# Attention and a PReLU layer on one core: alpha's load moved ahead of the second key load, one more tile stored token by token

## The chip, the core and the metric

The kernel runs on one core of a Trainium2 chip. A core has TensorE (PE: matrix multiplies and weight loads), VectorE (DVE), ScalarE (ACT), GpSimd (POOL) and SyncE (SP). Each engine works through its own list of instructions in order; between engines semaphores say when a result is there. SP and ACT also issue DMAs, the transfers between the chip's memory (HBM) and the core's memory (SBUF). PE writes its results to PSUM, eight banks of 128 x 512 float32, from which DVE and ACT fetch them.

The metric is the time of one execution in microseconds (us), measured on the device. Names with a number after a point, such as h9.10, are the kernel's own names for its steps and are explained below.

## What is computed

First comes attention with polynomial features: per row x, `phi(x)` is the outer product of two 8-vectors, S1 x and S2 x, 64 numbers. Its result, turned into 4352 tokens of 128 numbers, goes through two matrices with a PReLU between them.

```python
def phi(x):                                   # q, k, v: (4, 4, 1088, 32)
    a = np.einsum('rd,bhsd->bhsr', S1, x)     # S1, S2: (8, 32)
    b = np.einsum('rd,bhsd->bhsr', S2, x)
    return np.einsum('bhsi,bhsj->bhsij', a, b).reshape(*x.shape[:-1], r * r)
q_p, k_p = (phi(q), phi(k))
kv = np.einsum('bhsf,bhsd->bhfd', k_p, v)
z = np.sum(k_p, axis=2)
num = np.einsum('bhsf,bhfd->bhsd', q_p, kv)
den = np.einsum('bhsf,bhf->bhs', q_p, z)[..., None] + 1e-06
attn = num / den
x = attn.transpose(0, 2, 1, 3).reshape(4352, 128)
h = x @ w_in                                  # w_in: (128, 2048), alpha: (2048,)
g = np.maximum(h, 0.0) + alpha * np.minimum(h, 0.0)
out = g @ w_out                               # w_out: (2048, 128)
```

## The kernel before

**Stages.** Each of the four batches has a keys part and a queries part. Keys of batch 0: the key rows come in two loads (k0.0 of 18 rows per partition, k0.1 of 16), DVE transposes them (k0T0, k0T1, line 439), PE multiplies them by the features (k0f0, k0f1, line 473) with a weight tile `Wk` that DVE makes from S1 and S2, DVE turns the result back (k0fT1, k0fT0, line 477), POOL and DVE form the products (k0p0 to k0p4), and PE sums them: over the rows alone (zs00, zs01, line 504) and against v (kv00 to kv04, line 513). The sum zs goes through ACT (z10) and a small matmul (zS0, line 413) with the weight tile `S2q`, which itself is S2m on PE (line 329) and four ACT instructions (line 335); DVE then writes C0 into the weights of the queries. The queries of batch 0 are three pieces, qa0, qa1 (rows 0 to 15) and qb (the rest).

**The start.** Both S1 and S2 (1 KB each, into the tile `rows`) are needed before anything but transposes can run: rowsT (line 316) turns them on PE, DVE makes `Wk` and k0f0 follows. alpha (8 KB, tile `al`) is turned on PE by alT (line 340), much later.

**The second half.** x is cut into tiles: 0 and 1 of 256 tokens, 2 to 8 of 512, and tile 9 of 256 with the left-over tokens of all batches. For each tile g and each of 16 chunks c: h{g}.{c} is a matmul with a piece of `w_in` into a PSUM bank (line 628), r{g}.{c} is the relu from PSUM into a bfloat16 tile `rh`, on ACT (line 634) or DVE (line 636), and o{g}.{c} multiplies it by a piece of `w_out` scaled by 1 - alpha and sums over c in one bank. W{g} adds the linear part, x times w_in alpha w_out. A plain tile does o as one matmul of 512 columns with `w_a_bf` as weights (line 621); its result lies features by tokens, DVE transposes it in blocks of 32 (oT, line 654), and four stores st{g}.0 to .3 write 128-byte rows (line 664). Tile 8 is token-major: `rh` is the weight, four matmuls of 128 columns do the work (line 619), two copies of 256 columns (oT8.0, oT8.1) fetch it from PSUM, and four stores write 512-byte rows. Tile 9 does the same in two halves (line 616), with its own stores st9.0 to st9.2 from the tiles `of`.

**What sets the order.** Nothing is scheduled when the kernel is built: the table ORDER lists each step by name with its engine (p, a, d, g, s) and the PSUM banks or buffers it takes. A number behind p is a count of units of dummy work ahead of the step: `dummy` (line 294) issues matmuls of ones into bank 7, up to four units of 128 columns each, for no result. They fill PE while it waits.

**Waits of DMAs.** The DMAs of SP and ACT take eight completion semaphores, DMAHW0 to DMAHW7, in turn, in one order for both engines. A DMA that takes a semaphore first waits until the DMA that held it last, eight DMAs back, has landed. A DMA that waits holds up the queue of its engine.

```python
n = len(loads.setdefault(name, []))
o = op({e: 440 for e in eng}, emit, deps, name=f"ld_{name}" + (f"_{n}" if n else ""), nbytes=nbytes, rate=rate)
```

So `ld_rows` is S1, `ld_rows_1` is S2, and the four loads of v0 are ld_v0, ld_v0_1 to ld_v0_3, of which ld_v0_1 is issued last. SP's first DMAs are S2, S1, qb, w_in2, qa1, v0_3, v0, qa0, v0_2, v0_1.

Of the kernel before, what the change touches and what calls it, by code (L numbers as in the profile page):

```python
# [21 lines left out]


ORDER = """
ld_rows_1:s ld_rows:s ld_k0.0:a ld_k0.1:a ld_qb:s ld_alpha:a zero:d table:a ident:g identb:d selP:g ld_w_in2:s wz:g rowsT:p26:0 pads:g M2:d k0T0:d:0
Wk:d k0f0:p8:1 k0T1:d pads9:g Mh:d win2:a ld_qa1:s qbT:d ld_v0_3:s ld_v0:s M4:d k0f1:p1 k0fT1:d:0 k0fT0:d k0p0:g:0 zs00:p15:1 zs01:p ld_qa0:s ld_v0_2:s
z10:a:0 k0F1:d:2 k0p4:d S2m:p:3 S2q:a zS0:p15 qaT1:d qaT0:d ld_v0_1:s Wq:d k0p1:g ld_k2:s k0p2:d ld_w_out2:s C0:d alT:p:3 oma:d kv00:p1:4 alTc:a Wf:a
qcf:p:1 w_b2:g kv01:p kv02:p k0p3:d qcfc:a:0 qct:d:0 kv03:p kv04:p ld_w_in1:s qcrc:d:0 qcb:d qcp0:d:0 ld_w_in0:s ld_w_in3:s kvc0:a:0 qcPT0:d:0 qbf:p:2
qdf:p:0 qdfc:a:1 fin0:p kvR0:a ld_w_out1:s ld_k1:s qbfc:a:0 ld_k1_1:s w_a2:g ld_w_out0:s qdt:d:0 ld_k2_1:s win1:a win0:a ld_w_out3:s ld_q1_1:s ld_q1:s
# [33 lines left out]
r7.1:a:2 o8.11:p h7.12:p:2 st0.2:s o8.7:p r7.12:a:5 h9.3:p:3 o7.4:p o8.4:p r7.2:a:7 r7.10:d:0 o6.6:p oT6:d:3 h8.0:p:2 st6.0:s st6.1:s h8.1:p:5  # L63
r9.3:a:11 h8.5:p:6 r8.0:a:4 r8.1:d:3 o7.1:p o8.13:p st0.3:s h7.11:p:0 o7.2:p h9.6:p:2 o8.1:p st2.3:s h9.13:p:5 h8.10:p:3 r8.5:a:2 o8.5:p st0.1:s
r7.11:d:6 h9.14:p:0 r9.14:a:2 o7.11:p r8.10:d:3 h9.4:p:6 r9.4:a:6 h8.15:p:4 r8.15:d:7 o7.3:p o7.6:p h8.6:p:6 h9.9:p:0 o7.10:p r8.6:a:9 r9.9:d:10
o7.14:p o7.12:p oT7:d:1 o8.10:p h9.11:p:6 r9.13:d:3 o8.15:p h9.12:p:0 r9.6:a:1 h9.10:p:2 st6.3:s r9.10:a:7 o8.6:p h9.2:p:1 h9.0:p:4 st6.2:a o8.14:p
h9.7:p:2 r9.7:a:8 r9.11:d:9 o9.4:p:5 o9.10:p h9.1:p:3 r9.12:d:5 o9.3h:p r9.2:a:0 o9.9:p o8.0:p st7.3:s o9.10h:p h9.15:p:0 o9.12h:p h9.8:p:2 o9.4h:p
o9.3:p oT8.1:a:0 o9.12:p st7.2:s o9.6:p r9.1:d:4 h9.5:p:1 r9.15:d:6 o9.13:p st7.0:s st7.1:s r9.0:a:7 o9.7h:p r9.8:a:5 W9h:p r9.5:d:11 o9.2h:p o9.11:p
W9:p o9.11h:p o9.0:p oT8.0:a st8.0:s st8.2:a st8.1:s st8.3:s o9.7:p o9.1:p o9.2:p o9.1h:p o9.14:p o9.8:p o9.5:p o9.15:p oT9.0:d o9.6h:p o9.5h:p o9.8h:p
o9.0h:p o9.15h:p o9.9h:p st9.0:a o9.13h:p o9.14h:p oT9.1:d st9.1:s st9.2:a  # L70
"""


# [45 lines left out]
def kernel(  # L119
# [154 lines left out]
    ident = consts.tile([128, 128], F32, tag="ident", name="ident")  # L274
    identb = consts.tile([128, 128], BF16, tag="identb", name="identb")
    M4 = consts.tile([128, H], F32, tag="M4", name="M4")
    M2 = consts.tile([128, 2], F32, tag="M2", name="M2")
    selP = consts.tile([2 * r, 128], F32, tag="selP", name="selP")
    Wk = consts.tile([128, 2, 2 * r], F32, tag="Wk", name="Wk")
    Wf = consts.tile([128, B, 32], F32, tag="Wf", name="Wf")  # L280
    Mh = consts.tile([128, H], F32, tag="Mh", name="Mh")
# [70 lines left out]
    for i in range(NB):  # L352
        s = slice(4 * i, 4 * i + 4)
# [17 lines left out]
    for i in range(2):  # L371
        b = Buf("ps")
        s = slice(8 * i, 8 * i + 8)
# [292 lines left out]
    def store_main(b, lo, n):  # L666
        def st(g, o, boT):
            for i in range(4):
                put_out(g, i, [o], boT, bass.AP(tensor=out.tensor, offset=(b * S + lo // 32) * DM + 32 * i,
                                              ap=[[NJ * DM, 32], [DM, n // 32], [1, 32]]), lambda i=i: sb(boT)[32 * i:32 * i + 32, :n // 32])  # L670
        return st

    def store_token_major(b, lo):
        def st(g, os, boT):
            for i in range(4):
                dst = bass.AP(tensor=out.tensor, offset=(b * S + lo // 32 + i) * DM, ap=[[NJ * DM, 32], [4 * DM, 4], [1, DM]])
                put_out(g, i, os, boT, dst, lambda i=i: bview(sb(boT)[32 * i:32 * i + 32], [[DM, 4], [1, DM]]), 300.)
        return st
# [16 lines left out]
    last = len(tiles_)  # L695
    whole[last] = lambda: xr.rearrange("p y s b -> p (y s b)")
    for g, (b, lo, n, needs) in enumerate(tiles_):
        if g == last - 1:
            mlp(g, [(n, whole[g], needs)], store_token_major(b, lo), 1)
        else:  # L700
            mlp(g, [(n, whole[g], needs)], store_main(b, lo, n))
# [35 lines left out]
```

## Time and profile before

| what | value |
|---|---|
| three timed runs | 108.32, 111.84, 108.73 us; median 108.73 |
| the profiled execution, its own time | 108.08 us |
| its span, first to last instruction | 106.1 us |
| PE busy | 98.1 us, 92% |
| DVE, ACT, POOL busy | 80.3, 66.8, 44.6 us |
| HBM read, written | 8.79 MB, 2.23 MB |
| dummies (line 294), last matmul of PE | 27 matmuls, 9.3 us; 100.3 us |

Times within a profile count from the start of the span. The profile names engines as above; PEld is a weight load and runs beside PE, SPq and ACTq are DMA issues on the queues of SP and ACT. Its chain of waits goes back from the last instruction, at each step to what released it. In a timeline, `[1.34 <-DMA rows]` says that the engine was idle for 1.34 us before the row, and what ended that. Equal instructions that follow each other are one row with a count, xN. "us to landing" counts from the start of a DMA's issue until all of it has arrived.

### The profile page before, as it was taken

The page shows a single profiled execution, that of the slowest core. Times are in us where ns is not written, and L with a number is a line of the kernel's source. Part 1 is how long each engine was busy: PE and PEld are TensorE (multiplying, and loading weights), DVE is VectorE, ACT ScalarE, POOL GpSimd, SP SyncE. Part 2 cuts the span into 40 slices and gives each one's busy share as a digit, 9 for nine tenths or more (in the row PEclk, how much of TensorE's full clock was granted, in tenths as well). Part 3 has the DMA queues.
Part 4 walks back from the last instruction along what each step waited for, and adds up shares of the span by engine and source line. Part 5 has one row for each costly group of instructions (what it writes and reads, how often), then busy time and mean ns, then how long its engine had stood idle before and what let it go on. Part 6 is the DMA issues. An engine that isn't in the chain of part 4 may idle for free.

```text
span 106.1 us, 3513 instructions
## 1 busy us (share of the span) xinstructions
PE 98.1 (92%) x1462; PEld 54.8 (52%) x1462; DVE 80.3 (76%) x137; ACT 66.8 (63%) x156; POOL 44.6 (42%) x47
## 2 busy tenths in 40 slices
PE   7499999999999999999999999999999999999800
PEld 2124785766777644454444434654444464668700
DVE  3279589899889999779999773798686678688600
ACT  1421439998874984965769459797456945846500
POOL 7306535999955799990970005930100000000000
PEclk9999999999999999999999999999999999999998
DMA  2899999877980000380100000342000432053550
GB/s 65 287 297 269 308 335 308 288 211 242 254 197 20 0 0 6 78 228 21 25 0 6 12 0 0 54 77 48 6 0 0 74 62 49 6 90 57 106 136 12
DMA packets 23247, 11.24 MB, mean 106 GB/s; under 512 B 15664, under 2 KB 20800, under 8 KB 23232
## 3 DMA queue, kind: packets, MB, share of 16 engines
q1 hardware_dynamic: 18832, 9.84, 34.7%
q10 hardware_dynamic: 4400, 1.19, 4.8%
q8 instruction: 11, 0.18, 0.7%
q14 instruction: 4, 0.03, 0.2%
HBM read 8.79 MB, written 2.23 MB: 104 GB/s over the span
## 4 chain that ended last, share of the span: by engine, by line
PE 89%; DMA 3%; SPq 1%; issue 1%; DVE 0%; ACT 0%; ACTq 0%
PE ps L628 29%; PE ps L621 25%; PE ps L565 7%; PE ps L294 5%; PE ps L513 4%; PE ps L619 4%; DMA rows<-in_S_dram 3%; PE ps L473 3%; PE ps L534 2%; PE ps L390 2%; PE ps L616 2%; PE ps L429 1%; PE ps L504 1%; PE ps L380 1%; PE ps L403 1%; SPq L201 1%
## 5 line engine op out<-in xcount | busy, mean ns | idle before, releaser
L628 PE MATMUL ps<-x,w_in_bf 128*128 128x512 bf16 (+1 forms) x144 | 40.6, 356 | 0.0
L628 PEld LDWEIGHTS <-w_in_bf 128*128 128x128 bf16 x160 | 15.1, 98 | 13.3 <-issue 2.3
L621 PEld LDWEIGHTS <-w_a_bf 128*128 128x128 bf16 x128 | 12.4, 98 | 11.3 <-issue 1.6
L193 POOL TENSOR_TENSOR P__69<-Fk__67 128x512 f32<-128x512 f32 (+2 forms) x5 | 8.8, 1774 | 5.3 <-DVE Fk__67 L477 5.3
L294 PE MATMUL ps<-const-bfloat16-1.0 128*128 128x512 bf16 (+3 forms) x27 | 9.3, 475 | 0.8 <-PEq L721 0.8
L193 POOL TENSOR_TENSOR P__70<-F__66 128x1152 f32<-128x1152 f32 x4 | 8.6, 2170 | 2.7 <-DVE F__66 L193 2.7
L634 ACT ACTIVATE rh__88<-ps 128x512 bf16<-128x512 f32 (+1 forms) x12 | 6.1, 512 | 4.3 <-PE ps L628 2.7
L565 PE MATMUL ps<-Q__71,kvR 32*32 32x288 f32 (+2 forms) x384 | 7.7, 332 | 0.0
L634 ACT ACTIVATE rh__84<-ps 128x512 bf16<-128x512 f32 (+1 forms) x11 | 5.7, 519 | 2.7 <-DVE rh__86 L636 1.4
L634 ACT ACTIVATE rh__78<-ps 128x512 bf16<-128x512 f32 (+1 forms) x12 | 6.5, 545 | 1.2 <-PE ps L628 1.2
L634 ACT ACTIVATE rh__81<-ps 128x512 bf16<-128x512 f32 (+1 forms) x11 | 6.2, 565 | 1.4 <-PE ps L619 0.8
L558 DVE STREAM_TRANSPOSE Q__71<-P__70 128x1152 f32<-128x1152 f32 (+1 forms) x6 | 7.0, 1174 | 0.0
L634 ACT ACTIVATE rh__77<-ps 128x512 bf16<-128x512 f32 (+1 forms) x10 | 5.2, 517 | 1.6 <-PE ps L628 1.5
L634 ACT ACTIVATE rh__80<-ps 128x512 bf16<-128x512 f32 (+1 forms) x10 | 5.6, 564 | 0.8 <-PE ps L621 0.5
L565 PEld LDWEIGHTS ps<-Q__71,kvR 32*32 32x32 f32 x384 | 4.5, 103 | 2.9 <-ACT kvR L186 0.4
L186 ACT CAST x<-ps 128x576 bf16<-128x576 f32 (+2 forms) x8 | 4.0, 523 | 2.9 <-PE ps L565 2.9
L193 POOL TENSOR_TENSOR w_hl<-w_in_f,w_hl 128x512 bf16<-128x512 f32 x4 | 5.3, 1332 | 1.2 <-ACT w_hl L186 1.2
L634 ACT ACTIVATE rh__86<-ps 128x512 bf16<-128x512 f32 (+1 forms) x7 | 4.0, 570 | 2.8 <-PE ps L628 2.8
L634 ACT ACTIVATE rh__79<-ps 128x512 bf16<-128x512 f32 (+1 forms) x9 | 4.8, 531 | 1.3 <-PE ps L628 1.0
L432 DVE STREAM_TRANSPOSE F__66<-ps 128x1152 f32<-128x1152 f32 x3 | 4.2, 1383 | 1.6 <-PE ps L429 1.6
L193 POOL TENSOR_TENSOR P__69<-F__66 128x1152 f32<-128x1152 f32 x2 | 4.3, 2171 | 1.9 <-PE ps L628 1.9
L621 PE MATMUL ps<-rh__78,w_a_bf 128*128 128x512 bf16 (+1 forms) x14 | 5.1, 364 | 0.0
(191 smaller groups left out, 232.7 us busy)
## 6 DMA issues: line engine op xcount, KB each, us to landing
v<-in_v_dram SPq DMA_DIRECT2D x12, 144.0 KB, 3.6
k<-in_k_dram SPq DMA_DIRECT2D x6, 272.0 KB, 4.2
q<-in_q_dram SPq DMA_DIRECT2D x6, 272.0 KB, 4.2
w_in_f<-in_moe_w_in_dram SPq DMA_DIRECT2D x4, 256.0 KB, 4.5
w_out_f<-in_moe_w_out_dram SPq DMA_DIRECT2D x4, 256.0 KB, 4.6
out_dram<-oT__92 SPq DMA_DIRECT2D x10, 64.0 KB, 1.9
v<-in_v_dram SPq DMA_DIRECT2D x4, 112.0 KB, 3.8
out_dram<-oT__90 SPq DMA_DIRECT2D x5, 64.0 KB, 2.1
```

The lines of the kernel that those rows point to most:

```text
L186: nc.scalar.copy(dst, src)
L193: (nc.vector if e == "dve" else nc.gpsimd).tensor_tensor(out=dst, in0=a, in1=b, op=what)
L294: nc.tensor.matmul(PS[:, 7, :128 * m], ones(128), ones(128 * m), start=True, stop=True, skip_group_check=True)
L432: return op({"dve": V(4 * n) + 60}, lambda e: nc.vector.transpose(bview(sb(F), [[n, 4], [1, n]]), ps(bf)[:, :, :n]), [o1], [bf, F], name=f ...
L473: nc.tensor.matmul(dst, Wk[K].rearrange("p x f -> p (x f)"), col, start=True, stop=True, skip_group_check=not b)
L513: nc.tensor.matmul(ps(bk)[32 * h:32 * h + 32, :R], v_sb[b][:, h, j], bview(sb(P), [[1, R]], (4 * j + h) * R), start=j == 0, stop=j == JG - ...
L558: ts.append(op({"dve": V(R * n1) + 20}, lambda e, lo=lo, n1=n1: nc.vector.transpose(bview(sb(Q), [[1, R * n1]], lo * R), bview(sb(P), [[1, ...
L565: nc.tensor.matmul(ps(bn)[32 * h:32 * h + 32, g, :n], kvR[b][32 * g:32 * g + 32, y, 32 * h:32 * h + 32], bview(sb(Q)[32 * g:32 * g + 32], ...
L619: nc.tensor.matmul(ps(bo)[:, 128 * j:128 * j + 128], rhs[:, 128 * j:128 * j + 128], w, start=first and j == 0, stop=end, skip_group_check= ...
L621: nc.tensor.matmul(ps(bo)[:, :n], w, rhs, start=first, stop=end, skip_group_check=True)
L628: nc.tensor.matmul(ps(b)[:, lo:lo + m], w_in_bf[:, c], x(), start=True, stop=True, skip_group_check=len(parts) > 1)
L634: nc.scalar.activation(sb(br)[:, :n], ps(b)[:, :n], ACTF.Relu)
```

## The change

The change has four parts.

1. On ACT's queue alpha's load stands between the two first key loads instead of behind both.
2. The dummy counts: ahead of rowsT 30 instead of 26 units, ahead of k0f0 3 instead of 8, ahead of zs00 11 instead of 15.
3. Tile 7 is token-major as tile 8 is: its o steps use `rh` as weights, its transpose on DVE becomes two copies, oT7.0 on ACT and oT7.1 on DVE, and its stores write rows of 512 bytes.
4. The store st8.3 is issued by ACT instead of SP.

```diff
@@ -22,8 +22,8 @@
-ld_rows_1:s ld_rows:s ld_k0.0:a ld_k0.1:a ld_qb:s ld_alpha:a zero:d table:a ident:g identb:d selP:g ld_w_in2:s wz:g rowsT:p26:0 pads:g M2:d k0T0:d:0
...
+ld_rows_1:s ld_rows:s ld_k0.0:a ld_alpha:a ld_k0.1:a ld_qb:s zero:d table:a ident:g identb:d selP:g ld_w_in2:s wz:g rowsT:p30:0 pads:g M2:d k0T0:d:0
...
@@ -695,7 +695,7 @@
     for g, (b, lo, n, needs) in enumerate(tiles_):
-        if g == last - 1:
+        if g >= last - 2:
             mlp(g, [(n, whole[g], needs)], store_token_major(b, lo), 1)
         else:
             mlp(g, [(n, whole[g], needs)], store_main(b, lo, n))
```

**At the start.** ACT's first instructions before: the two key loads (`k0_103`), alpha (`al_99`), then the table load and what follows.

```order
L201 DMA k0_103<-in_k_dram 128x576
L201 DMA k0_103<-in_k_dram 128x512
L201 DMA al_99<-in_moe_alpha_dram 16x128
L286 ACT_TABLE_LOAD
L286 ACTIVATE tab_125<-tab_125 128x1
```

The same in the changed kernel.

```order
L201 DMA k0_103<-in_k_dram 128x576
L201 DMA al_99<-in_moe_alpha_dram 16x128
L201 DMA k0_103<-in_k_dram 128x512
L286 ACT_TABLE_LOAD
L286 ACTIVATE tab_125<-tab_125 128x1
```

alpha's load and the second key load have changed places; SP's list of DMAs is as it was.

PE from rowsT (L316) to the first features of the keys (L473) and on to the dummies (L294) ahead of zs00, before and now as one difference.

```order
 L316 MATMUL ps<-ident,rows 32x16 x4
 L294 LDWEIGHTS const-bfloat16-1.0
-L294 MATMUL ps<-const-bfloat16-1.0 128x512
-L294 LDWEIGHTS const-bfloat16-1.0
-L294 MATMUL ps<-const-bfloat16-1.0 128x512
+L294 MATMUL ps<-const-bfloat16-1.0 128x384
 L473 MATMUL ps<-T__64,Wk 32x72x2 x8
 L294 LDWEIGHTS const-bfloat16-1.0
 L294 MATMUL ps<-const-bfloat16-1.0 128x128
 L473 MATMUL ps<-T__64,Wk 32x72x2 x8
```

Between rowsT and k0f0 stand 384 dummy columns where 1024 stood. Ahead of zs00 one dummy matmul of 512 columns is gone, and ahead of rowsT one more stands.

**At the end.** SP's last stores before, with the semaphores each waits for: four of tile 7 (`oT1__90`), three of tile 8 (`oT0__89`: st8.0, st8.1, st8.3) and st9.1 (`of1_139`). A bare DMAHW is the one that the store then takes itself.

```order
L664 DMA out_0_dram<-oT1__90 32x16x32 [waits DMAHW0_49,DVE_49]
L664 DMA out_0_dram<-oT1__90 32x16x32 [waits DMAHW3_49]
L664 DMA out_0_dram<-oT1__90 32x16x32 [waits DMAHW5_49]
L664 DMA out_0_dram<-oT1__90 32x16x32 [waits DMAHW6_49]
L664 DMA out_0_dram<-oT0__89 32x4x128 [waits DMAHW7_49,Activation_49]
L664 DMA out_0_dram<-oT0__89 32x4x128 [waits DMAHW0_49]
L664 DMA out_0_dram<-oT0__89 32x4x128 [waits DMAHW1_49]
L685 DMA out_0_dram<-of1_139 16x4x128 [waits DMAHW2_49,DVE_49]
```

The same in the changed kernel.

```order
L664 DMA out_0_dram<-oT1__90 32x4x128 [waits DMAHW0_49,DVE_49]
L664 DMA out_0_dram<-oT1__90 32x4x128 [waits DMAHW2_49]
L664 DMA out_0_dram<-oT1__90 32x4x128 [waits DMAHW4_49]
L664 DMA out_0_dram<-oT1__90 32x4x128 [waits DMAHW6_49]
L664 DMA out_0_dram<-oT0__89 32x4x128 [waits DMAHW0_49,Activation_49]
L664 DMA out_0_dram<-oT0__89 32x4x128 [waits DMAHW1_49]
L685 DMA out_0_dram<-of1_139 16x4x128 [waits DMAHW2_49,DVE_49]
```

SP has one store of tile 8 fewer, and the stores take other semaphores. Before, DMAHW5 of the third row was held last by st6.2, DMAHW1 by st8.2 and DMAHW2 by st9.0, all three issued by ACT. Now DMAHW1 of st8.1 was held last by st8.2, and DMAHW2 of st9.1 by the second store of tile 7.

ACT's end, the two places at which it changed, as one difference: the copy oT7.0 ahead of r9.6 (`rh1__78`), and the stores st8.2, st8.3, st9.0, st9.2.

```order
 L634 ACTIVATE rh9__86<-ps_63 128x512 [waits PE_49]
-L634 ACTIVATE rh1__78<-ps_63 128x256 [waits PE_49]
+L186 COPY oT1__90<-ps_63 128x256 [waits DMAHW4_49,DMAHW3_49,DMAHW7_49,DMAHW0_49,PE_49]
+L634 ACTIVATE rh1__78<-ps_63 128x256
 L634 ACTIVATE rh7__84<-ps_63 128x256 [waits DVE_49,PE_49]
```

```order
 L664 DMA out_0_dram<-oT0__89 32x4x128 [waits DMAHW1_49,Activation_49]
-L685 DMA out_0_dram<-of0_138 32x4x128 [waits DMAHW2_49,DVE_49]
-L685 DMA out_0_dram<-of1_139 16x4x128 [waits DMAHW4_49,DVE_49]
+L664 DMA out_0_dram<-oT0__89 32x4x128
+L685 DMA out_0_dram<-of0_138 32x4x128 [waits DMAHW5_49,DVE_49]
+L685 DMA out_0_dram<-of1_139 16x4x128 [waits DMAHW7_49,DVE_49]
```

The copy stands ahead of the relu r9.6, which frees the PSUM bank of h9.6 for h9.10. st8.3 stands between st8.2 and st9.0 and waits for nothing of its own.

More of the change, by code (lines that the diff above doesn't have):

```diff
@@ L24 @@
 ORDER = """
-ld_rows_1:s ld_rows:s ld_k0.0:a ld_k0.1:a ld_qb:s ld_alpha:a zero:d table:a ident:g identb:d selP:g ld_w_in2:s wz:g rowsT:p26:0 pads:g M2:d k0T0:d:0
-Wk:d k0f0:p8:1 k0T1:d pads9:g Mh:d win2:a ld_qa1:s qbT:d ld_v0_3:s ld_v0:s M4:d k0f1:p1 k0fT1:d:0 k0fT0:d k0p0:g:0 zs00:p15:1 zs01:p ld_qa0:s ld_v0_2:s
+ld_rows_1:s ld_rows:s ld_k0.0:a ld_alpha:a ld_k0.1:a ld_qb:s zero:d table:a ident:g identb:d selP:g ld_w_in2:s wz:g rowsT:p30:0 pads:g M2:d k0T0:d:0
+Wk:d k0f0:p3:1 k0T1:d pads9:g Mh:d win2:a ld_qa1:s qbT:d ld_v0_3:s ld_v0:s M4:d k0f1:p1 k0fT1:d:0 k0fT0:d k0p0:g:0 zs00:p11:1 zs01:p ld_qa0:s ld_v0_2:s
 z10:a:0 k0F1:d:2 k0p4:d S2m:p:3 S2q:a zS0:p15 qaT1:d qaT0:d ld_v0_1:s Wq:d k0p1:g ld_k2:s k0p2:d ld_w_out2:s C0:d alT:p:3 oma:d kv00:p1:4 alTc:a Wf:a
@@ L65 @@
 r7.11:d:6 h9.14:p:0 r9.14:a:2 o7.11:p r8.10:d:3 h9.4:p:6 r9.4:a:6 h8.15:p:4 r8.15:d:7 o7.3:p o7.6:p h8.6:p:6 h9.9:p:0 o7.10:p r8.6:a:9 r9.9:d:10
[L66 to L70, printed above, removed]
+o7.14:p o7.12:p oT7.0:a:1 oT7.1:d o8.10:p h9.11:p:6 r9.13:d:3 o8.15:p h9.12:p:0 r9.6:a:1 h9.10:p:2 st6.3:s r9.10:a:7 o8.6:p h9.2:p:1 h9.0:p:4 st6.2:a
+o8.14:p h9.7:p:2 r9.7:a:8 r9.11:d:9 o9.4:p:5 o9.10:p h9.1:p:3 r9.12:d:5 o9.3h:p r9.2:a:0 o9.9:p o8.0:p st7.3:s o9.10h:p h9.15:p:0 o9.12h:p h9.8:p:2
+o9.4h:p o9.3:p oT8.1:a:0 o9.12:p st7.2:s o9.6:p r9.1:d:4 h9.5:p:1 r9.15:d:6 o9.13:p st7.0:s st7.1:s r9.0:a:7 o9.7h:p r9.8:a:5 W9h:p r9.5:d:11 o9.2h:p
+o9.11:p W9:p o9.11h:p o9.0:p oT8.0:a st8.0:s st8.2:a st8.1:s st8.3:a o9.7:p o9.1:p o9.2:p o9.1h:p o9.14:p o9.8:p o9.5:p o9.15:p oT9.0:d o9.6h:p o9.5h:p
+o9.8h:p o9.0h:p o9.15h:p o9.9h:p st9.0:a o9.13h:p o9.14h:p oT9.1:d st9.1:s st9.2:a
 """
```

## The prediction

> **What bounds the kernel now.** I read the page first, then the waits, then the chain of waits in order of time, and last the queues of SP and ACT at both ends of the span. The page's chain gives PE nearly everything, and the waits of PE name one stall worth a line:
>
> ```profile
> PE 89%; DMA 3%; SPq 1%; issue 1%; DVE 0%; ACT 0%; ACTq 0%
> ```
> ```profile
> PE ps L316 <- DMA rows<-in_S_dram: 1.3, 1, 1.3
> ```
>
> So PE has no hole from 5.04 us until its last matmul; what is not PE lies ahead of 5.04 and behind it. The chain in order of time (start, length, what), from S1's load to the first dummies:
>
> ```profile
> 1.63 3.27 DMA rows<-in_S_dram
> 4.91 0.14 issue
> 5.04 0.30 PE ps L316 x8
> 5.34 0.97 PE ps L294 x2
> ```
>
> From k0f1 (L473) to the dummies ahead of zS0, then kv00, then four dummies from later on:
>
> ```profile
> 7.19 0.66 PE ps L473 x16
> 7.86 1.71 PE ps L294 x4
> 9.57 0.35 PE ps L504 x17
> 9.92 0.41 PE ps L329 x2
> 10.34 0.92 PE ps L294 x4
> ```
> ```profile
> 11.80 0.36 PE ps L513 x16
> ```
> ```profile
> 15.65 0.87 PE ps L294 x4
> ```
>
> S1 is issued at 1.63 and lands at 4.90; rowsT (L316) starts on it. L294 are dummies: 0.97 us of them stand ahead of k0f0, which so starts at 6.31, 1.71 ahead of zs00 (L504), 0.92 ahead of zS0. They also show the clock: 15 units of 128 columns take 1.71 us at 7.86, 16 units 0.87 at 15.65. PE runs at half rate until zs00 and at full rate from there, some 4.6 us after it took up unbroken work at 5.04.
>
> The queues that feed this stretch (start, length), and landings counted from the start of an issue:
>
> ```profile
> 0.73 1.54 SPq L201 DMA_DIRECT2D rows<-in_S_dram  x2
> 2.32 0.44 SPq L201 DMA_DIRECT2D q<-in_q_dram  x1
> ```
> ```profile
> 5.88 1.25 SPq L201 DMA_DIRECT2D v<-in_v_dram  x2
> ```
> ```profile
> 0.75 0.88 ACTq L201 DMA_DIRECT2D k<-in_k_dram  x2
> 1.66 0.69 ACTq L201 DMA_DIRECT2D al<-in_moe_alpha_dram  x1
> ```
> ```profile
> k<-in_k_dram ACTq DMA_DIRECT2D x1, 288.0 KB, 2.7
> k<-in_k_dram ACTq DMA_DIRECT2D x1, 256.0 KB, 3.1
> ```
> ```profile
> q<-in_q_dram SPq DMA_DIRECT2D x1, 288.0 KB, 3.8
> ```
> ```profile
> v<-in_v_dram SPq DMA_DIRECT2D x1, 144.0 KB, 3.6
> ```
>
> k0.1 starts at about 1.19 and lands at 4.3; qb lands at 2.32 + 3.8 = 6.1; the last of the four v0 loads starts at about 6.5 and lands at 10.1. These landings don't move with PE. DVE on this stretch, with its idle time before a row in brackets:
>
> ```profile
> 5.40 0.19 DVE L320 TENSOR_TENSOR Wk<-ps,M 128x32 f32<-128x32 f32 x1 [1.11 <-PE ps L316]
> 5.51 0.70 DVE L439 STREAM_TRANSPOSE T__64<-k 128x512 f32<-128x512 f32 x1
> ```
> ```profile
> 6.30 0.67 DVE L595 STREAM_TRANSPOSE qTb<-q 128x480 f32<-128x480 f32 x1
> ```
> ```profile
> 7.96 0.85 DVE L477 STREAM_TRANSPOSE Fk__67<-ps 128x320 f32<-128x320 f32 x2 [0.67 <-PE ps L473]
> ```
>
> At the end, the stores. SP's last two, ACT's last three, how long a store of 64 KB takes to land, and the last DVE copy of the chain:
>
> ```profile
> 101.80 0.32 SPq L664 DMA_DIRECT2D out_dram<-oT__89  x1
> ```
> ```profile
> 102.74 0.63 SPq L685 DMA_DIRECT2D out_dram<-of  x1
> ```
> ```profile
> 99.55 0.32 ACTq L664 DMA_DIRECT2D out_dram<-oT__89  x1
> 100.20 1.32 ACTq L685 DMA_DIRECT2D out_dram<-of  x2
> ```
> ```profile
> out_dram<-oT__90 SPq DMA_DIRECT2D x2, 64.0 KB, 2.0
> ```
> ```profile
> 100.32 0.29 DVE of L188
> ```
>
> st9.1 goes out at 102.74, though its data, that DVE copy, was ready at 100.61. It waited for its semaphore DMAHW2, last held by st9.0 of 100.20; and st8.3 ahead of it, at 101.80, for DMAHW1, held by st8.2 of 99.55. Nothing of the program starts after st9.1, so the span ends a fixed time behind it.
>
> **The change, part by part.**
>
> *S1 and alpha.* ACT issues alpha second and k0.1 third: k0.1 starts 0.69 us later, at about 1.9, behind S1's start at 1.63 instead of ahead of it. No row prices S1's landing without k0.1 ahead. One end is no gain, 4.90 again (or 0.2 later, if alpha ahead of it costs something). The other is set by PE itself: the dummies ahead of rowsT grow from 26 units to 30, at 1.71 / 15 = 0.114 us a unit from 0.77 to 4.2, and before that rowsT can't start. The nearest rows are the two key loads issued beside it, 2.7 and 3.1 from their start; S1 is small and right behind the first, so I take 1.63 + 2.7 = 4.3, hence rowsT at 4.4 where it stood at 5.04. The longer dummies hide.
>
> *k0f0 and k0f1.* The dummies behind rowsT fall from 8 units to 3, 0.34 us, less than the 0.55 between rowsT's start and Wk's end (5.04 to 5.59): k0f0 starts at 4.4 + 0.6 = 5.0 instead of 6.31. k0T1 takes 0.70 behind Wk, if k0.1 has landed by then. k0.1's bounds are 4.3 (it was queued behind k0.0's packets anyhow) and 1.9 + 3.1 = 5.0; I take 4.9. So k0T1 ends at 5.65, k0f1 runs 5.7 to 6.4, against 7.19 to 7.86.
>
> *What is late next.* DVE's order is k0T1, Mh, qbT, M4, k0fT1. qbT needs qb, which lands at 6.1. From qbT's start to M4's end it is 0.99 (6.30 to 7.96 less the 0.67 of idling), so k0fT1 can't start before about 7.15, nor the two k0fT end before 8.0 (0.85). That gains 0.8 us where PE had gained 1.45. zs00's dummies go from 15 units to 11 (1.25 us from 6.4, ended at 7.65): hidden, and zs00 starts at 8.05 where it stood at 9.57. Here DVE's 0.8 and the removed wait behind the dummies (9.57 - 8.81 = 0.75) add up to 1.5.
>
> *From zs00 on.* zs, S2m, S2q on ACT and zS0 keep their distance if PE is at full rate: zS0 stood at 10.34 + 0.92 = 11.26, 1.69 behind zs00, and kv00 0.54 behind it. So zS0 at 9.75, kv00 at 10.3. kv00 also needs all four v0 loads, landed at 10.1: the gain is capped at 11.80 - 10.15 = 1.65, and 1.5 is within it. Alpha's own use (alT) comes after zS0, long past any landing. From kv00 on the chain is PE throughout. After this stretch the waits of DVE, ACT and POOL name a load only once, and that for 0.2 us:
>
> ```profile
> POOL P__70 L193 <- DMA w_out_f<-in_moe_w_out_dram: 0.2, 1, 0.2
> ```
>
> POOL is off the chain there. I cost later loads at nothing, and the 1.5 us stays to the end. Bounds of this part: 0.8 (no gain by S1, dummies alone, rival B) and 1.65, or some 1.9 if v0 too comes earlier.
>
> [...]
>
> *Tile 7 token-major.* Seventeen single matmuls of 512 columns become 17 x 4 of 128 columns, each with its own weight load. The chain prices both kinds where they stand side by side:
>
> ```profile
> 84.21 0.22 PE ps L619 x4
> 84.43 0.22 PE ps L621
> ```
>
> To the second decimal no difference; 17 x 0.005 = 0.1 us at most. The 0.72 us transpose on DVE becomes two copies, one on ACT, one on DVE:
>
> ```profile
> 96.00 0.38 ACT L634 ACTIVATE rh__78<-ps 128x256 bf16<-128x256 f32 x1
> ```
> ```profile
> 96.22 0.72 DVE L654 STREAM_TRANSPOSE oT__90<-ps 128x512 f32<-128x512 f32 x1 [0.22 <-PE ps L621]
> ```
> ```profile
> 96.57 0.38 PE L628 MATMUL ps<-xr,w_in_bf 128*128 128x256 bf16 x2
> ```
>
> ACT's copy can't start before 96.22 and stands ahead of r9.6, which ran at 96.00 and is of the same size (0.38). r9.6 now ends near 96.9 instead of 96.4, and h9.10, the second of the two PE rows at 96.57, needs its PSUM bank at 96.7. That is a new wait of 0.2 (0 to 0.38). Together with the matmuls I put 0.25 us on PE's end, 0.1 of which DVE's freed 0.35 may give back.
>
> *The stores.* The four st7 now follow semaphores that stores of 92 to 95 us held last, of which this is the latest:
>
> ```profile
> 95.01 0.45 SPq L664 DMA_DIRECT2D out_dram<-oT__92  x1
> ```
>
> With 2.0 to land they are all free by 97.1, so the st7 go out between 96.65 and 98.5 without a wait. st8.3 moves to ACT, so SP has st8.0, st8.1, st9.1. st8.1 waits on DMAHW1 for st8.2, as st8.3 did; st9.1 on DMAHW2 for a st7, long landed, so no longer for st9.0. st8.2 goes at 99.55 + 0.25 = 99.8 and lands 2.0 later: st8.1 at 101.8, st9.1 right behind at 102.2 instead of 102.74. Gain 0.5; bounds: 0.25 (2.25, as the rows show for st8.2 with two st7 moving beside it) or even 0 with more issues at once, and 0.8 (1.7). I take 2.0, since the st7 have landed by then. The 512-byte rows get no term: 64 KB in rows of 128 bytes land in 2.0, st8.2 in rows of 512 held SP for 2.25.
>
> **The sum.** 1.5 + 0.5 = 2.0 us. The profiled execution took 108.08 (span 106.1): 106.1. That profile is 0.6 below the median of 108.73, so against the median it would be 2.4%.
>
> **The rivals.**
>
> *B, S1 lands no earlier.* For it: S1 and k0.1 are issued by different engines. Then rowsT stays at 5.04; k0f0 starts at 5.65, k0f1 ends at 7.2, 11 dummies last to 8.4, and zs00 gains 1.17. If the clock still turns near 9.6, S2m at half rate costs 0.4 of it: 0.8 + 0.5, 106.8. [...] Against it: S1's 1 KB took 3.27 us to land, longer than the 288 KB of k0.0 (2.7), so something stood ahead of it.
>
> *C, a load takes S1's place.* k0.1 now moves while qb should. If qb and v0 land 0.6 later, the start gains 0.9: 106.7.
>
> *D, the tail pays nothing.* st8.2's landing replaces st9.0's in full: 106.6.
>
> *E, both ends.* v0 earlier and the tail at its best: 108.08 - 1.9 - 0.8 = 105.4.
>
> *F, slower.* PE is idle for 0.4 us before zs00, and the dummies that kept it busy are fewer. If this holds the clock at half rate, each us of it costs half a us from zs00 at 8.05 on; it eats the 2.0 us if it lasts past 12.05, and until 14 gives 108.08 - 2.0 + 3.0 = 109.1. Against it: before, a hole of 1.34 us was followed by a turn 4.6 us later, and the new holes are shorter.
>
> **How the numbers follow.** Chances: forecast 0.46, B 0.15, C 0.12, D 0.12, E 0.11, F 0.04. Likeliest: 106.1. C with D gives 107.2, and runs of one kernel differ by 0.4 (108.32 and 108.73), which I add half of at the upper end and all of at the lower: 105.0 to 107.4. It leaves out F and the far ends, under 2 in 10. 2% of the times shown is 2.17 us, about what a measurement of this kernel can tell from no change. The forecast stands on that edge (2.0 against the profiled run, 2.6 against the median): of A some 0.34 counts as faster, with E and a little of the rest 0.50; the others stay within 2%, 0.47; of F and unknown mishaps 0.03 is slower by more.
>
> **What would show it.** Right: rowsT near 4.4, qbT waiting for q, the k0fT near 7.15, zs00 near 8, kv00 near 10.3, st9.1 following st8.1 at once. Wrong: rowsT at 5.0 (B), kv00 held by v after 10.6 (C), st9.1 as late behind PE's end as before (D), dummies near 0.43 us per 512 columns after zs00 (F), or a PE hole in the middle that eats the 1.5.

## The result and the profile after

| what | before | after |
|---|---|---|
| median on the same chip | 108.53 us (107.85 to 111.84, 4 runs) | 111.65 us (111.15 to 111.94, 4 runs) |
| profiled execution, its span | 108.08, 106.1 us | 111.15, 109.2 us |

The changed kernel is slower: the ratio of the times is 1.030, with an interval of 1.024 to 1.037. Forecast were 106.1 us, and 105.0 to 107.4. A ratio here and below leaves out the runs that lie over 1.5% above the fastest run of their kernel (the 111.84 of the kernel before is one), so the median and spread of all runs stand beside it.

S1 does land earlier: by 4.21, where it had landed at 4.90. In the timeline of the changed kernel (start, length, engine, line, what) rowsT stands right behind its 30 dummies, and k0f0 follows at full rate (0.53 us; k0f1, further down, takes 0.73):

```profile
4.21 0.25 PE L316 MATMUL ps<-ident,rows 16*32 16x16 f32 x8
...
4.76 0.53 PE L473 MATMUL ps<-T__64,Wk 64*32 64x144 f32 x16
```

Then PE stops. The waits of the changed kernel have a row that the kernel before didn't have (total, times, longest), and the timelines of PE and DVE show its place:

```profile
PE ps L473 <- DVE T__64 L439: 2.0, 1, 2.0
```
```profile
6.55 0.71 DVE L439 STREAM_TRANSPOSE T__64<-k 128x512 f32<-128x512 f32 x1 [1.85 <-DMA k<-in_k_dram]
...
7.41 0.73 PE L473 MATMUL ps<-T__64,Wk 64*32 64x144 f32 x16 [1.95 <-DVE T__64 L439]
```

k0f1 waits for k0T1, and k0T1 for k0.1. The issues of the two loads (KB, us from issue to landing) show that k0.1 took 4.9 where it had taken 3.1, and qb 4.4 where it had taken 3.8:

```profile
k<-in_k_dram ACTq DMA_DIRECT2D x1, 256.0 KB, 4.9
```
```profile
q<-in_q_dram SPq DMA_DIRECT2D x1, 288.0 KB, 4.4
```

The chain of waits of the changed kernel from that load to fin0 (line 403, the end of the key sums of batch 0):

```profile
1.66 4.88 DMA k<-in_k_dram
6.53 0.03 issue
6.55 0.72 DVE T__64 L439
...
8.48 0.95 PE ps L294 x2
9.44 0.46 PE ps L504 x18
9.90 0.72 PE ps L329 x2
10.62 1.71 PE ps L294 x4
...
12.99 0.58 PE ps L513 x16
13.58 1.10 PE ps L534 x4
14.68 1.65 PE ps L513 x56
16.33 2.37 PE ps L534 x14
18.70 0.22 PE ps L403 x2
```

The same end in the chain of the kernel before:

```profile
15.43 0.22 PE ps L403 x2
```

The late load has cost nothing at zs00 (L504) against the kernel before: it starts at 9.44, 0.13 ahead, where 1.5 had been forecast. The loss lies behind it. From zs00 to fin0 PE took 9.26 us where it had taken 5.86. No wait stands there; the same work is slower. S2m (L329) takes 0.72 instead of 0.41, the 15 units of dummies ahead of zS0 1.71 instead of 0.92, kv00 (L513) 0.58 instead of 0.36. The windows show the clock (stretch, its length, PE busy with the count, granted clock, DMA share, GB/s):

```profile
7.00:7.50 0.50, 0.09 (x8) 0.88 0.97 301
9.40:17.40 8.00, 8.00 (x116) 0.50 0.92 291
17.50:18.00 0.50, 0.50 (x6) 0.88 1.05 352
```

A mean of 0.88 over half a us that starts at 1.00 and ends at 0.50 means that the clock fell at 7.38, and by the same working it rose again at 17.62. In between it was 0.50 with PE busy all the time from 9.4 on. The fall stands at the end of the hole of 1.95 us. This record alone isn't enough: in the kernel before it stands at 1.00 from the start, also while the dummies ran at half rate by their durations (1.71 us for 15 units), so the duration of a like row is the safer sign.

From fin0 on nothing more is lost until tile 7: the last fin stands at 74.18 against 70.91, again 3.27 later. The end of the program (chain, then the queue of SP, then its waits):

```profile
103.96 0.29 DVE of L188
```
```profile
103.18 2.62 SPq L664 DMA_DIRECT2D out_dram<-oT__89  x2
105.90 0.63 SPq L685 DMA_DIRECT2D out_dram<-of  x1
```
```profile
SPq L664 <- DMA out_dram<-oT__89: 2.0, 1, 2.0
```

The last DVE copy is 3.64 later than before, so tile 7 costs 0.37. From that copy's end to the span's end it is 4.95 us instead of 5.49, so the stores give 0.54. In the chain r9.6 on ACT now stands among the rows of PE, part of tile 7's cost; the row of ACT's queue is st8.2 and st8.3:

```profile
99.88 0.40 ACT rh__78 L634
```
```profile
103.18 1.18 ACTq L664 DMA_DIRECT2D out_dram<-oT__89  x2
```

In all -0.13 + 3.40 + 0.37 - 0.54 = 3.10 us, which is the difference of the spans.

### The profile page after: what moved, and what is told of

The parts are those of the page before. It is cut to its first block, busy times and chain, and to the rows that moved or that the text cites. A ratio compares the mean times of both kernels' runs of the same rounds, so it can differ in the third digit from the quotient of the medians.

```text
span 109.2 us, 3603 instructions
## 1 busy us (share of the span) xinstructions
PE 99.5 (91%) x1498; PEld 59.1 (54%) x1512; DVE 80.1 (73%) x137; ACT 67.1 (61%) x157; POOL 44.6 (41%) x47
## 3 DMA queue, kind: packets, MB, share of 16 engines
HBM read 8.79 MB, written 2.23 MB: 101 GB/s over the span
## 4 chain that ended last, share of the span: by engine, by line
PE 79%; DMA 4%; DVE 4%; POOL 4%; issue 2%; ACTq 1%; ACT 1%
PE ps L628 26%; PE ps L621 18%; PE ps L619 7%; PE ps L565 5%; PE ps L513 5%; DMA k<-in_k_dram 4%; PE ps L294 4%; POOL P__69 L193 4%; PE ps L534 3%; PE ps L390 2%; PE ps L473 2%; PE ps L616 2%; PE ps L429 1%; DVE Q__71 L558 1%; PE ps L504 1%
## 5 line engine op out<-in xcount | busy, mean ns | idle before, releaser
L628 PE MATMUL ps<-x,w_in_bf 128*128 128x512 bf16 (+1 forms) x139 | 39.5, 355 | 0.7 <-issue 0.3
L621 PEld LDWEIGHTS <-w_a_bf 128*128 128x128 bf16 x112 | 10.9, 98 | 10.0 <-issue 1.6
L294 PE MATMUL ps<-const-bfloat16-1.0 128*128 128x512 bf16 (+3 forms) x23 | 8.6, 500 | 1.3 <-PEq L721 0.8
L193 POOL TENSOR_TENSOR P__70<-F__66 128x1152 f32<-128x1152 f32 x4 | 8.6, 2173 | 2.7 <-DVE F__66 L193 2.6
L294 PEld LDWEIGHTS <-const-bfloat16-1.0 128*128 128x128 bf16 x26 | 2.8, 119 | 4.8 <-issue 4.2
L439 DVE STREAM_TRANSPOSE T__64<-k 128x576 f32<-128x576 f32 (+2 forms) x3 | 2.8, 930 | 3.2 <-DMA k<-in_k_dram 3.2
```

Source lines behind the costliest of these rows:

```text
L193: (nc.vector if e == "dve" else nc.gpsimd).tensor_tensor(out=dst, in0=a, in1=b, op=what)
L294: nc.tensor.matmul(PS[:, 7, :128 * m], ones(128), ones(128 * m), start=True, stop=True, skip_group_check=True)
L621: nc.tensor.matmul(ps(bo)[:, :n], w, rhs, start=first, stop=end, skip_group_check=True)
L628: nc.tensor.matmul(ps(b)[:, lo:lo + m], w_in_bf[:, c], x(), start=True, stop=True, skip_group_check=len(parts) > 1)
```

## The experiments

Theory K says that the hole ahead of k0f1 sends PE to half rate for some 10 us, and that this is the loss. Its rivals: L, the late load costs time by itself; D, the dummy counts do it; T, tile 7 does it. The ratios are against the kernel before on the same chip.

**Each part alone.** The first kernel has only alpha's load moved:

```diff
-ld_k0.0:a ld_k0.1:a ld_qb:s ld_alpha:a
+ld_k0.0:a ld_alpha:a ld_k0.1:a ld_qb:s
```

> The kernel before with alpha's load alone moved between the two key loads; dummies and tile 7 as before. Theory K (clock): the second key load lands near 6.5 instead of 4.3, PE then has a hole of 1.3 to 1.5 us ahead of k0f1, and PE runs at half rate for some 10 us from there; the start loses 2.5 to 3.5 us: about 111. Rival L (the load itself): the late load shifts k0f1 by 0.2 us and nothing more: 108 to 109. Rival D (the dummy counts do it): 108 to 108.5, the loss comes with the dummies.

The second has only the dummy counts: rowsT:p30, k0f0:p3, zs00:p11.

> The kernel before with the three dummy counts alone (30, 3, 11). K: no key load is late, so the only hole is the one ahead of rowsT, shorter than the 1.3 us of before; the clock behaves as before: 107.3 to 108.5. D: with 9 units fewer behind rowsT PE is not busy enough and stays at half rate: 110.5 to 112.

The third has only tile 7 and st8.3 (`if g >= last - 2`, st8.3:a). The fourth is the whole change without alpha's move.

> The kernel before with tile 7 token-major and st8.3 on ACT alone. K: the second half loses about 0.35 us on PE (the copy on ACT ahead of r9.6) and gains 0.55 behind PE's end: 108.3, 0.2 below the kernel before. Rival T (token-major costs PE more than the chain shows): 109 or more.

> The changed kernel without the move of alpha's load. K: the whole loss is gone: each of the two other parts gave 0.3 to 0.5% less than the kernel before, so 107.5 to 108. If the parts need each other (the dummy counts were laid out for the early S1), 109 or more.

| kernel | median, runs | ratio, interval |
|---|---|---|
| alpha_only | 111.49 (110.97 to 112.26, 4) | 1.027, 1.020 to 1.034 |
| dummies_only | 108.50 (107.03 to 110.67, 10) | 0.995, 0.990 to 1.001 |
| tile7_only | 108.51 (107.11 to 111.07, 10) | 0.997, 0.991 to 1.002 |
| dummies_tile7 | 109.84 (107.28 to 111.99, 10) | 1.002, 0.996 to 1.007 |

Alpha's move alone makes the loss, with all the old dummies in place, and in all four runs. D and T fall as its cause. In alpha_only's timeline and windows the hole and the half rate are there again:

```profile
7.53 0.73 PE L473 MATMUL ps<-T__64,Wk 64*32 64x144 f32 x16 [1.97 <-DVE T__64 L439]
```
```profile
7.00:7.50 0.50, 0.00 (x0) 0.52 1.03 300
17.00:17.50 0.50, 0.50 (x4) 0.74 0.89 281
```

The clock falls at 7.02 and rises at 17.26: 10.24 us, as in the changed kernel (7.38 to 17.62). The fewer dummies are not harmless either: four of the ten runs of dummies_only lie at 110.0 us and above (none of the 25 of the kernel before on that chip), and five of the ten of dummies_tile7 at 110.7 and above, five at 109.0 and below, so that its median misses the expected 107.5 to 108. The profile of dummies_tile7, of 107.58 us, shows a hole ahead of zs00, 1.5 us long, with full rate before and after it (k0f1 0.54 us, S2m 0.41):

```profile
8.92 0.38 PE L504 MATMUL ps<-Fk__67 128*32 128x32 f32 x18 [1.49 <-DVE Fk__67 L477]
```

That the slower runs of both kernels lost the clock there would fit K and rival F of the prediction, but no profile of one was taken.

**The hole filled, the load as late.** The changed kernel with 30 units of dummies ahead of k0f1 instead of 1:

```diff
-k0f1:p1
+k0f1:p30
```

> The changed kernel with 30 units of dummies instead of 1 ahead of k0f1, so that PE has little or no hole while it waits for the second key load; no load is moved. K: the clock is at full rate from about 4 us on and stays there; k0f1 at 7.4, kv00 near 11: 107.5 to 109. L: nothing changes for the loads, 111 to 112. If the clock has not turned by k0f1, the dummies last 3.2 us and k0f1 comes at 8.5: then 109 to 110.

Measured: 108.46 us (107.08 to 109.86, 10 runs), ratio 1.000, 0.995 to 1.005. The chain of its profile:

```profile
6.00 3.32 PE ps L294 x8
9.31 0.74 PE ps L473 x16
...
10.98 0.38 PE ps L504 x18
...
13.24 0.36 PE ps L513 x16
...
16.86 0.22 PE ps L403 x2
```

The dummies now last past the transpose of k0.1, so that k0f1 and zs00 come 1.9 and 1.5 us later than in the changed kernel, kv00 0.25 us later. Yet fin0 comes 1.84 earlier, since PE goes from zs00 to fin0 in 5.88 us. This tells L and K apart: with k0.1 as late, and PE delayed on top, 3 us come back in the median when the hole is filled, and all ten runs stay below the four of the changed kernel. The profile is of the longest of the ten, 109.86 us. In it PE was not yet at full rate when k0f1 ran (0.74 us), the third case of the expectation, and reached it by zs00 (0.38). So it shows that without the hole the full rate comes and stays; a profile in which the full rate came first and the dummies then kept it wasn't taken.

**A hole made without moving a load.** Here the loads are as before. On DVE k0T1 is put behind Mh, qbT and M4, so that k0f1 waits for it:

```diff
-Wk:d k0f0:p8:1 k0T1:d pads9:g Mh:d win2:a ld_qa1:s qbT:d ld_v0_3:s ld_v0:s M4:d k0f1:p1
+Wk:d k0f0:p0:1 pads9:g Mh:d win2:a ld_qa1:s qbT:d ld_v0_3:s ld_v0:s M4:d k0T1:d k0f1:p1
```

> The kernel before with no load moved, but DVE's transpose k0T1 put behind Mh, qbT and M4, and no dummies ahead of k0f0, so that PE has a hole of some 1.6 us ahead of k0f1 for a reason that is no DMA. Theory K (a hole there sends PE to half rate for some 10 us): 110.5 to 112. Rival L (only a late load does that; here k0f1 comes 0.8 later and nothing else): 108.5 to 109.5.

The same with 14 units ahead of k0f1, and then with 30:

> The same, with 14 units of dummies instead of 1 ahead of k0f1, so that the hole is filled and nothing else differs. K: the clock turns as in the kernel before: 108 to 109.5, some 2 us below the run without the filling. L: no difference between the two.

> late_kT1 again (no load moved, k0T1 behind M4 on DVE), now with 30 units of dummies ahead of k0f1 instead of 14: 30 units last 3.4 us at half rate and 1.7 at full rate, so PE should have no hole of more than about half a us between k0f0 and k0f1 in either state. Theory K (the hole sends PE to half rate for some 10 us): the runs form one group at 107.7 to 110 us, ratio 1.00 to 1.015, and the profile shows full rate from about 9 us on and fin0 at 17.5 or earlier. Theory L (a late k0T1 costs what it costs, whatever the clock): 112 to 113 as late_kT1, ratio 1.035 to 1.05. A third way: the hole is filled and the clock still falls, then holes elsewhere or the way PE was fed decide it, and K is wrong as stated.

| kernel | median, runs | ratio, interval |
|---|---|---|
| late_kT1 (1 unit) | 112.99 (112.25 to 114.79, 4) | 1.047, 1.039 to 1.055 |
| late_kT1_fill (14) | 111.76 (107.74, 111.44, 112.08, 113.08) | none |
| late_kT1_fill2 (30) | 108.97 (108.57 to 109.78, 10) | 1.007, 1.004 to 1.011 |

The rows of the three timelines of PE at k0f1, in this order, the first with k0f0 too:

```profile
5.21 0.74 PE L473 MATMUL ps<-T__64,Wk 64*32 64x144 f32 x16 [0.30 <-DVE Wk L320]
...
8.26 0.74 PE L473 MATMUL ps<-T__64,Wk 64*32 64x144 f32 x16 [2.08 <-DVE T__64 L439]
```
```profile
5.54 0.94 PE L294 MATMUL ps<-const-bfloat16-1.0 128*128 128x512 bf16 x4
8.01 0.73 PE L473 MATMUL ps<-T__64,Wk 64*32 64x144 f32 x16 [1.54 <-DVE T__64 L439]
```
```profile
6.15 3.38 PE L294 MATMUL ps<-const-bfloat16-1.0 128*128 128x512 bf16 x8
9.46 0.55 PE L473 MATMUL ps<-T__64,Wk 64*32 64x144 f32 x16
```

The kernel with a hole of 2.08 us is 4.7% slower, more than K's 110.5 to 112 us, though no load has moved; with the hole filled it is 0.7%, and all ten runs lie between 108.57 and 109.78. From zs00 to fin0 it is 9.45 us (10.71 to 20.16) in the first and 5.88 (11.03 to 16.91) in the third, though the third starts zs00 later. So a hole ahead of k0f1 brings the long half rate in a kernel that has none of the change in it. But K's wording is too narrow: in the first of the three, k0f0, which stands ahead of the hole, took 0.74 us and so ran at half rate already. There the hole did not end a full rate, it put off its coming: by the chain, whose fourteen matmuls of line 534 at 17.60 took 2.56 us instead of 1.73, the clock turned near 19.3, an estimate from these rows, where in the kernel before it turned near 9.6.

The middle one missed what it was made for. Its 14 units were to last 1.6 us at half rate. In the profiled run the clock had already turned, so they took 0.94 us and left a hole of 1.54. The windows of that run:

```profile
6.50:7.00 0.50, 0.00 (x0) 0.88 1.08 370
17.00:17.50 0.50, 0.50 (x18) 0.89 0.98 268
```

Half rate from 6.88 to 17.11 is 10.23 us, the third time the same. The fall at 6.88 lies only 0.40 us into the hole (6.48 to 8.01), so the length of this hole can't be all that decided it; shorter ones, of 0.87 and 0.30 us, stood ahead of it. One of its four runs took 107.74, so that this kernel too is not the same in each run.

**Why k0.1 landed late.** K starts from a load that came 2.2 us later though its issue moved by 0.47 us. Either it shares the DMA engines with qb and what follows on SP (Q), or alpha's load ahead of it on ACT's queue holds it up (A). The kernel is alpha_only, with SP's loads from qb on held back until DVE has done k0T0, by a small write into qb's place:

```diff
-ld_qb:s zero:d table:a ident:g identb:d selP:g ld_w_in2:s wz:g rowsT:p26:0 pads:g M2:d k0T0:d:0
+zero:d table:a ident:g identb:d selP:g wz:g rowsT:p26:0 pads:g M2:d k0T0:d:0 qz:d ld_qb:s ld_w_in2:s
...
+c_qz = op({"dve": 60}, lambda e: nc.vector.memset(q_sb[0][:, 16:17], 0.0), name="qz")
-load_rows("qb", q_sb[0][:, 16:], q, 0, 16, NJ - 16)
+load_rows("qb", q_sb[0][:, 16:], q, 0, 16, NJ - 16, [c_qz])
```

> alpha_only with one thing more: a small write on DVE behind k0T0 into the place that qb will fill, so that SP issues qb, and all its loads behind it, only after k0T0 (about 4.3 us instead of 2.3). k0.1 keeps its place behind alpha. Theory Q (k0.1 lands late because it shares the 16 DMA engines with qb): k0.1 lands at 4.7 to 5.2 us where it landed at 6.5 to 6.7. Theory A (it lands late because alpha's load stands ahead of it on ACT's queue, whatever SP does): 6.0 us or later. The time itself says little, since qb and v0 come some 2 us later: by theory K it may lose the clock at another hole.

The timeline of ACT's queue, SP's and DVE:

```profile
1.65 0.69 ACTq L201 DMA_DIRECT2D k<-in_k_dram  x1
...
4.69 0.37 SPq L201 DMA_DIRECT2D q<-in_q_dram  x1
...
5.19 0.71 DVE L440 STREAM_TRANSPOSE T__64<-k 128x512 f32<-128x512 f32 x1 [0.44 <-DMA k<-in_k_dram]
```

k0.1 now lands at about 5.15 (3.5 from its issue), with alpha still ahead of it: Q, within the expected 4.7 to 5.2. Of the 1.8 us by which it took longer (4.9 against 3.1) 1.4 come back; what the other 0.4 are, alpha's load ahead or another, stays open. In the kernel before k0.1 was issued 1.13 us ahead of qb, in the changed one 0.66. The time, 110.74 us (one run), says little, for qb and v0 were late. But its PE rows show that a hole of 2 us is not the only way to a late full rate: k0f0 and k0f1 ran at half rate (0.73 each), behind the first matmul the longest hole up to fin0 was 0.71 us, ahead of zs00, and yet PE took 8.68 us from zs00 to fin0.

**The end.** In the kernel before, only st8.3 goes to ACT:

```diff
-st8.3:s
+st8.3:a
```

> The kernel before with st8.3 issued by ACT and nothing else changed. Theory S1 (the end depends on which store holds the semaphore that st9.1 takes): st9.1 now follows st8.3 on DMAHW2 instead of st9.0, SP no longer waits at st8.3, and the span behind PE's last copy falls from 5.5 to about 5.0: ratio 0.993 to 0.998. Rival S2 (the gain at the end came from the 512-byte rows of tile 7's stores): the span behind PE's last copy stays 5.4 to 5.6, ratio 0.998 to 1.002.

Measured: 106.89 us (106.15 to 108.40, 10 runs), ratio 0.989, 0.985 to 0.993. The chain's last row, st8.2 and st8.3 on ACT, and SP's last stores:

```profile
101.04 0.29 DVE of L188
```
```profile
100.27 0.86 ACTq L664 DMA_DIRECT2D out_dram<-oT__89  x2
```
```profile
100.26 2.29 SPq L664 DMA_DIRECT2D out_dram<-oT__89  x2
102.65 0.63 SPq L685 DMA_DIRECT2D out_dram<-of  x1
```

From the copy's end to the span's end (106.0) it is 4.67 us instead of 5.49: 0.8 us from one letter in the table. That this span is no shorter than before has another cause: its profiled run, of 108.04 us, is one of the longest of the ten, and PE stands idle once in batch 1 where in the kernel before it doesn't, for nothing that the profile names:

```profile
33.67 1.10 PE L513 MATMUL ps<-P__69,v 128*32 128x64 f32 x63 [0.72 <-issue]
```

S1 holds, and S2 falls: the gain needs no 512-byte rows. It is larger than S1 had put it, since it has two parts. st9.1 now follows the store ahead of it on SP by 0.41 us (102.24 to 102.65) instead of 0.94 (101.80 to 102.74), as its wait for st9.0 is gone: 0.53. And the store that waits for st8.2 (st8.1 now, an issue of 0.32 us at the end of SP's pair) starts 1.97 us behind st8.2's issue instead of 2.25: 0.28, whose cause is open. The edit gives st9.1 another semaphore and takes a store off SP's queue at once; no run parts the two. With the 512-byte rows tile 7's own stores land a little sooner (median 1.8 us against 2.0 in the kernel before), but the end is worse, 5.51 in tile7_only and 4.95 in the changed kernel. SP's st8.1 waits for st8.2 to land, 1.6 us in st83_only, 2.0 in the changed kernel, 2.5 in tile7_only. Why st8.2 lands later beside tile 7's wider rows wasn't tried.

The next kernel is tile7_only with both copies of tile 7 on DVE:

```diff
-oT7.0:a:1 oT7.1:d
+oT7.0:d:1 oT7.1:d
```

> The kernel before with tile 7 token-major and st8.3 on ACT, but both copies of tile 7 on DVE, so that ACT's r9.6 has nothing new ahead of it. Theory T1 (the 0.36 us that PE's end lost came from ACT's copy standing ahead of r9.6, and from DVE's copy waiting for ACT's): 0.3 us better than tile7_only, ratio 0.990 to 0.995 against the kernel before. Rival T2 (it came from the 68 small matmuls with their weight loads): as tile7_only, ratio 0.995 to 0.999, with the o rows of tile 7 longer on PE.

The row of its DVE timeline, and of SP's waits:

```profile
96.11 0.76 DVE L188 COPY oT__90<-ps 128x256 f32<-128x256 f32 x2 [0.24 <-PE ps L619]
```
```profile
SPq L664 <- DMA out_dram<-oT__89: 2.4, 1, 2.4
```

Measured: 108.01 us (107.43 to 111.64, 10 runs), ratio 0.998, 0.994 to 1.002. By the time this is T2, but the chain says that each theory has a part. From the last fin to the last copy PE and DVE take 29.41 us in the kernel before (70.91 to 100.32), and just as much in alpha_only, dummies_only and late_kT1, 29.78 in tile7_only and the changed kernel, and 29.55 in tile7_dve. So having a copy on ACT, ahead of r9.6, costs 0.23, and 0.14 stays for the rest of tile 7's edit; that this is the small matmuls is not shown. The 0.23 is less than the runs' spread, and the late end (5.48) keeps the time where it was.

**Better than both.** The kernel before with 38 units ahead of rowsT instead of 26 and nothing else:

> The kernel before with 38 instead of 26 units of dummies ahead of rowsT, which fills the hole of 1.3 us in which PE waits for S1. K: PE is busy from 0.8 us on, the clock turns at 4 to 7.6 instead of 9.6, and zs00 comes some 0.5 to 0.7 us earlier: 107.3 to 108. Rival (the hole does nothing, and dummies that outlast S1 by up to 0.3 us hold up rowsT): 108.5 to 109.

It took 107.90 us (106.89 to 109.55, 10 runs), ratio 0.997, 0.991 to 1.002. Its profile, of 107.16 us, has fin0 1.2 us earlier (14.24), but the median moves little. In it PE was at full rate by rowsT at 4.76 (0.25 us, then k0f0 in 0.53); no profile with these 38 units shows a turn as late as the expectation's 7.6. Then with qbT behind k0fT0 on DVE, tile 7 as in tile7_dve and st8.3 on ACT (best1), and last the same without tile 7 (best2), whose diff is:

```diff
-rowsT:p26:0
+rowsT:p38:0
...
-ld_qa1:s qbT:d ld_v0_3:s ld_v0:s M4:d k0f1:p1 k0fT1:d:0 k0fT0:d k0p0:g:0
+ld_qa1:s ld_v0_3:s ld_v0:s M4:d k0f1:p1 k0fT1:d:0 k0fT0:d qbT:d k0p0:g:0
...
-st8.3:s
+st8.3:a
```

> Candidate to beat both kernels: loads in the old order, 38 units of dummies ahead of rowsT instead of 26, qbT behind k0fT0 on DVE, tile 7 token-major with both copies on DVE, st8.3 on ACT. Theory: no hole ahead of k0f1, so full rate from about 8 us or earlier; k0fT1 no longer waits behind qbT for qb; 0.3 to 0.5 us of the end: 106.5 to 107.5 us, ratio 0.985 to 0.995. Rival: the runs split into two groups at the start as in dummies_tile7, and the median is no better than before, ratio 0.995 to 1.005.

> The kernel before with three edits that do not touch the loads or tile 7: 38 units of dummies ahead of rowsT instead of 26, qbT behind k0fT0 on DVE, st8.3 on ACT. Theory: the start of best1 (kv00 near 10.3) and the end of st83_only (4.7 us behind PE's last copy instead of 5.5) add up: 105.8 to 106.9 us, ratio 0.980 to 0.990. Rival: an earlier start only meets a later load of batch 1, so that it is no better than st83_only: ratio 0.988 to 0.993.

best1 took 107.59 us (106.53 to 108.59, 12 runs), ratio 0.993, 0.990 to 0.996; best2 106.70 us (106.00 to 107.84, 12 runs), ratio 0.990, 0.986 to 0.995. best1 lies within its theory's ratio. best2 beats both kernels, but its median by no more than st83_only, whose one edit gives 0.989: the ratio is in the rival's range, though the interval reaches into the theory's. The rival's reason, a later load of batch 1, doesn't show in best2's profile, of 106.18 us: fin0 is 1.00 earlier than in the kernel before and the last fin still 0.99 (69.92), and with the end of 4.68 us both gains add up there. What held its start is v0 (chain; kv00 follows at 10.73):

```profile
6.67 3.92 DMA v<-in_v_dram
```

## Why the prediction was wrong

- *S1 ahead: right.* rowsT was put at 4.4 and stood at 4.21, k0f0 at 5.0 and stood at 4.76. B falls. But part of it is the profile compared with: in the twelve profiles with the loads in the old order rowsT stands anywhere from 4.51 (late_kT1_fill) to 5.04, in the four with alpha ahead of k0.1 from 4.15 to 4.60.
- *k0.1's landing: the step that failed first.* It was put at 4.9, with 5.0 as the upper bound (1.9 + 3.1), from a row in which k0.1 was issued 1.13 us ahead of qb. It landed at 6.53; alpha_qb_wait shows that most of the delay comes from qb and the loads behind it on SP. Rival C spoke of k0.1 moving while qb should, and qb did land 0.6 later, as C had it; what C left out is the same delay for k0.1. A bound by the longest row seen isn't a bound when the change puts the transfer beside another.
- *k0f1: therefore at 7.41 instead of 5.7.* Of the 1.5 us expected at zs00, 0.13 was left.
- *The clock: the step that made the sign.* "zs, S2m, S2q on ACT and zS0 keep their distance if PE is at full rate", and full rate was taken for granted once it was reached. That PE is at full rate from zs00 on, which the 1.5 us needs, no run of the changed kernel shows: in its profile full rate was reached by k0f0 (0.53 us at 4.76) and lost again at 7.38, so that zS0 and kv00 didn't keep their distance: kv00 came 3.55 us behind zs00 instead of 2.23. In after_fill's profile k0f1 still ran at half rate at 9.31 (0.74 us), though PE had no hole above 0.5 us behind its first matmul. Rival F had this mechanism, placed it ahead of zs00 and gave it 0.04, with the reason that a hole of 1.34 us had done no harm before. That hole lay at 3.70, ahead of any full rate (the 26 units before it took 2.93 us, 0.113 each, as at half rate), so it could not show a loss.
- *F's time comes out by luck.* At half a us for each us of half rate from 8.05 on, until 17.62, it gives 108.08 - 2.0 + 4.8 = 110.9; the profiled run took 111.15. But two errors cancel: zs00 gained 0.13 instead of 1.5, and the half rate cost 3.40 instead of 4.8, as it met zs00 only from 9.44 and at 0.42 us for each us. Two of the signs named as "wrong" in the prediction came: dummies near half rate (15 units in 1.71 us, 0.46 for 512 columns), and a hole in the middle.
- *Tile 7: the mechanism right, the size a little low.* 0.37 us instead of 0.25: 0.23 for ACT's copy (put at 0.2) and 0.14 for the rest (the matmuls were put at 0.1).
- *The stores: the mechanism right, the size too large.* The forecast 0.5 is what is left after tile 7's 0.25 (st9.1 at 102.2 instead of 102.74). What was left is 0.54 - 0.37 = 0.17. st9.1 did follow st8.1 at once (0.42 us). The mis-sized term is st8.2's landing, put at 2.0 us: st8.1, which waits for it, started at 105.48 (the 0.32 us at the end of SP's pair), 2.30 behind st8.2's issue at 103.18, near the 2.25 that the row of the kernel before had shown. In st83_only, without the wider rows, it was 1.97; the prediction had no term for these rows.

## What to carry to other kernels

A load's row from issue to landing belongs to the transfers that ran beside it: k0.1's was 3.1 us in the kernel before, 4.9 in the changed one and 3.5 in alpha_qb_wait. Before a load is moved by half a us, look at what the other queue issues in that half us. A hole in PE can have a price beyond its length: here one of 1.95 us was followed by a loss of 3.4 us in rows with no wait, so compare the duration of the same row on both sides of a hole. Where the wait can't be avoided, dummies can fill it, but their count must be laid out for the full rate: 14 units, counted at half rate, left 1.54 us open in the profiled run, while with 30 units none of twenty runs of two kernels took more than 109.9 us.

## What the runs showed of the hardware

- After a fall the half rate lasted the same time in all three profiles that show one: 10.24 us in the changed kernel, 10.24 in alpha_only and 10.23 in late_kT1_fill, while PE had no hole from 8.48, 8.60 and 9.08 on. In two profiles at half rate from the start, with no fall on record, the full rate came near 19.3 (late_kT1) and 16.3 (alpha_qb_wait), estimates from the durations.
- The clock fell in holes of 1.54, 1.95 and 1.97 us (late_kT1_fill, the changed kernel, alpha_only), 0.40, 1.92 and 1.46 us after they began. In the changed kernel 9.1 us of unbroken work (8.48 to 17.62) stood ahead of the turn to full rate.
- A hole of 1.54 us in late_kT1_fill came with the loss of the clock, one of 1.49 in dummies_tile7 did not. What decides it, and why alpha_qb_wait came to full rate late with no hole above 0.71 us, stays open.
- Dummies are no clock: 14 units take 1.6 us at half rate (an estimate from the 15 units in 1.71) and took 0.94 in a run where the clock had turned.
